# A chain of three layers on one core: when the second feed-forward layer's weights are loaded, joined and stored while the first one runs

## The chip, the cores and the metric

The kernel runs on one core of a Trainium2 chip. The metric is the device time of one execution in microseconds (us). TensorE (PE, with its weight loads as PEld) multiplies matrices, VectorE (DVE), ScalarE (ACT) and GpSimd (POOL) do elementwise work, SyncE (SP) issues nearly all DMAs from one queue, in program order.

## The reference

Three layers follow one another: an attention with positive features, a feed-forward layer with g = h cos h, and a feed-forward layer with g = relu(h)².

```
phi(x)  = concat(exp(p - m), exp(-(p - m)))   with p = x @ w_phi, m = max|p|
attn    = phi(q) (phi(k)^T v) / (phi(q) sum(phi(k)) + 1e-6)     # 4 x 8 heads, 576 tokens of 64
x       = attn as 2304 tokens x 512
h = x @ moe_w_in  (512 -> 2048);  x = (h * cos(h)) @ moe_w_out  (2048 -> 512)
h = x @ moe2_w_in (512 -> 2048);  out = relu(h)**2 @ moe2_w_out (2048 -> 512)
```

All weights of the two feed-forward layers arrive as 64-bit floats, which the chip's engines don't compute with. The kernel reads them as pairs of 32-bit words and makes 32-bit floats of them; those it splits into a high and a low part, and each product is three matmuls (high x high, high x low, low x high).

## The kernel before, in words

**Order of the layers.** Attention fills the first 175 us. The first feed-forward layer follows in five blocks of tokens, of 512, 256, 512, 512 and 512 tokens (blocks 0 to 4). The second feed-forward layer takes the rest; it forms its first product with seven products instead of eight (line 615, its elementwise work from L632 on) and its second one at L670.

**A block of the first layer.** `feed_forward` goes through 16 + 3 steps i. Step i issues G1 of chunk i (12 matmuls, L313 to L315), then elementwise work of chunks i and i-1, then G2 of chunk i-3 (12 matmuls, L385). Elementwise: ScalarE rounds (A1: L327, L328), VectorE reduces the argument (A2: L330, L332), ScalarE takes sine and square (B1: L334, L335), VectorE forms h cos h (B2: L337), ScalarE makes its high part g (B3: L342) and VectorE the low part (B4: L345). `g` has two buffers, freed by G2. At the end of a block `split_x` splits the next block's tokens (L299, L303).

**Conversion of a weight tile** (128 rows x 512 values, 512 KB). A load (L472) brings the words. `w_words` takes the magnitude of one word (ACT, L239, into `mag`, three buffers) and scales the other in place (ACT, L241). `w_join` clamps (DVE, L257), shifts (DVE, L259), adds the two words (POOL, L261) and puts in the sign (DVE, L267). For the first product of the second layer, pairs of tiles are combined to the sums that its seven products want (`combine`, POOL, L511). `spill_split` makes the high part (ACT, L531) and the low part (DVE, L532) in a staging area, and SyncE stores it to DRAM (L533). The second layer reads it back (L493, and `read_out` at L502).

**What sets the order.** Each engine works in program order. `ahead()` lists events for tiles of the second layer, each with a due time `at`: load, words, joins, splits. `converts(j, i)` advances a clock by the matmul time that the step of block j adds (about a microsecond of TensorE per unit; 12 matmuls at 512 columns count 2.72) and, at the end of each step of blocks 1 to 3, issues all events due by then. Twenty tiles are treated so: the 16 of `w_in` and 4 of `w_out`; the other 12 of `w_out` (`late_outs`) are converted during the second layer and stay on chip. Loads alternate between two areas in the upper rows of the buffer `xbuf` (`areas(0)`, `areas(1)`), the staging areas are one slot of the weight pool (`st`) and `areas(2)`, `areas(3)`. Areas 0 and 2, and 1 and 3, lie in the same rows, and a load, a conversion or a split that touches one waits for what still reads or writes the other.

Of the kernel before, what the change touches and what calls it, by code (L numbers as in the profile page):

```python
# [31 lines left out]
AHEAD_TILES = (  # L32
    ("out", 0), ("out", 1), ("in", 0), ("in", 1), ("in", 2), ("in", 3), ("out", 2), *(("in", n) for n in range(4, 8)),
    ("out", 3), *(("in", n) for n in range(8, 16)),
)
AHEAD_FIRST, AHEAD_NEXT, AHEAD_STAGE = (0.0, 11.0, 22.0, 33.0), 9.7, 5.5
# [128 lines left out]
def attention_ffn_kernel(  # L165
# [11 lines left out]
    nc = tc.nc  # L177
# [15 lines left out]
    with tc.manual_schedule():  # L193
# [58 lines left out]
        def w_join(layer, n, step):  # L252
            m = mag_t[layer, n]
            mi = m.bitcast(I32)
            word0, word1 = raw_t[layer, n]
            if step == 0:
                nc.vector.tensor_scalar(out=m, in0=m, scalar1=F64_MIN, scalar2=F64_MAX, op0=ALU.max, op1=ALU.min)  # L257
            elif step == 1:
                nc.vector.tensor_scalar(out=mi, in0=mi, scalar1=3, scalar2=None, op0=ALU.logical_shift_left)  # L259
            elif step == 2:  # L260
                soon(layer, n).tensor_tensor(out=halves(mi), in0=halves(mi), in1=word0, op=ALU.add)  # L261
            else:
                raw_t.pop((layer, n))
# [256 lines left out]
        def spill_split(src, to, at):  # L520
            n = staged[0] % (3 if at >= 47.0 else 1)
# [11 lines left out]
            nc.sync.dma_start(out=to, in_=st[:, :, 0:w])  # L533

        def split_piece(p, i, at):
# [6 lines left out]
            spill_split(src, spilled(p, i), at)  # L542

        def stages(t, at, d, load, split):
            p = t[1] // 2
            yield at - d, lambda: load(t)
            yield at, lambda: [w_words(1, t, i) for i in range(2)]
            yield at + d, lambda: [w_join(1, t, i) for i in range(3)]
            yield at + 2 * d, lambda: w_join(1, t, 3)
            if t[0] == "out":  # L550
                yield at + 3 * d, lambda: split(t, at + 3 * d)
            elif t[1] % 2:
                yield at + 2 * d, lambda: combine(p)
                yield at + 3 * d, lambda: [split_piece(p, i, at + 3 * d) for i in (0, 3)]
                yield at + 4 * d, lambda: [split_piece(p, i, at + 4 * d) for i in (1, 2)]

        def ahead():
            events = []
            for n, t in enumerate(AHEAD_TILES):
                at = AHEAD_FIRST[n] if n < 4 else AHEAD_FIRST[3] + AHEAD_NEXT * (n - 3)  # L560
# [4 lines left out]
                def split(t, at):  # L565
                    spill_split(mag_t.pop((1, t)), out_spill(t[1]), at)

                events += stages(t, at, AHEAD_STAGE, load, split)
            return sorted(events, key=lambda e: e[0])

        def late_outs():
            events = []
            for n in range(4, KFF):
# [4 lines left out]
                def split(t, at):  # L578
                    w_split(1, t, 0)
                    w_split(1, t, 1)  # L580

                events += stages(("out", n), 9 + (n - 4) * 3.0, 2, load, split)
            return sorted(events, key=lambda e: e[0])

# [134 lines left out]
        def second_layer():  # L719
            events = late_outs()  # L720
            for s in range(1, NG * NP + 1):
                for k in range(7):
                    second_step(s, k)
                    while events and events[0][0] < 7 * s + k + 1:
                        events.pop(0)[1]()
# [10 lines left out]
        def behind_last(i):  # L736
# [7 lines left out]
            elif i >= 10 and i % 2 == 0 and i < 18:  # L744
                read_out((i - 10) // 2)
# [386 lines left out]
```

## Time and profile before

| | |
|---|---|
| median of 3 runs | 997.62 us (997.43 to 997.94) |
| profiled execution | 999.31 us, its span 997.5 us |
| TensorE busy | 968.7 us, 97% of the span, 5865 matmuls |
| VectorE, ScalarE, GpSimd busy | 66%, 59%, 17% |
| mean granted clock of TensorE | 0.988 |

TensorE is busy nearly throughout. A busy TensorE at its lower clock does half as much, so its busy share alone doesn't tell what is lost: the profile's slices of the span show 97% busy and a few slices in which busy share or granted clock is 8 tenths, between 270 and 530 us. That is where the first layer's blocks 1 to 3 run with the conversions of the second layer's weights among them. The rows below cover that stretch and what follows it.

### The profile page before, as it was taken

What the parts mean: (1) busy time and instruction counts of PE and PEld (TensorE: products, weight loads), DVE (VectorE), ACT (ScalarE), POOL (GpSimd) and SP (SyncE); (2) the same over time, 40 slices, a digit from 0 to 9 for tenths busy, and PEclk for the clock granted to TensorE, in tenths of its full rate; (3) what the DMA queues carried; (4) which work ended last, traced back from release to release, by engine and by line L of the source; (5) the groups of instructions that cost most, each with busy time, mean ns of one, the idle gap of its engine ahead of it and who ended that gap; (6) DMA issues with size and microseconds to landing.
All of it is one profiled execution on the core that took longest, in us unless ns stands there. A gap on an engine that the chain in (4) does not pass through costs nothing.

```text
span 997.5 us, 15678 instructions
## 1 busy us (share of the span) xinstructions
PE 968.7 (97%) x5865; PEld 831.8 (83%) x5865; DVE 661.7 (66%) x1136; ACT 585.2 (59%) x1145; POOL 171.1 (17%) x146
## 2 busy tenths in 40 slices
PE   8999999999979999899989999999999999999998
PEld 8888888788879788678868888898888888898887
DVE  6787887599846767777676754678774434743444
ACT  4988887699757766776676663455443223432223
POOL 1665863000001223223210000122100000000000
PEclk9999999999989999899989999999999999999999
DMA  7567632322023233354234502765644435453311
GB/s 253 160 203 223 209 106 78 111 105 76 14 72 106 75 139 117 136 168 137 97 141 152 171 1 74 249 205 180 204 147 146 120 118 156 155 166 109 117 53 63
DMA packets 54459, 132.46 MB, mean 133 GB/s; under 512 B 6512, under 2 KB 12272, under 8 KB 54384
## 3 DMA queue, kind: packets, MB, share of 16 engines
q1 hardware_dynamic: 54240, 131.41, 40.8%
q8 instruction: 46, 0.75, 0.3%
q14 instruction: 29, 0.24, 0.1%
q10 hardware_dynamic: 144, 0.07, 0.0%
HBM read 105.09 MB, written 26.29 MB: 132 GB/s over the span
## 4 chain that ended last, share of the span: by engine, by line
PE 45%; DVE 4%; ACT 4%; DMA 2%; issue 1%; POOL 1%; SPq 0%; DVEq 0%; ACTq 0%; POOLq 0%
PE acc L670 19%; PE m L615 17%; PE acc L385 5%; PE h L315 1%; PE h L314 1%; PE h L313 1%; DMA xbuf<-in_dram 1%; DVE tr L330 1%; DMA sp<-xbuf 1%; ACT tr L334 1%; ACT tr L327 1%; ACT tr L328 1%; DVE xr L445 0%; DVE tr L332 0%; DVE xc L452 0%
## 5 line engine op out<-in xcount | busy, mean ns | idle before, releaser
L385 PE MATMUL acc<-g,w 128*128 128x512 f32 (+1 forms) x960 | 221.6, 380 | 18.9 <-ACT g L342 13.6
L670 PE MATMUL acc<-w,g 128*128 128x512 f32 x864 | 226.0, 394 | 0.0
L385 PEld LDWEIGHTS acc<-g,w 128*128 128x128 f32 x960 | 173.1, 195 | 56.5 <-ACT g L342 16.0
L670 PEld LDWEIGHTS acc<-w,g 128*128 128x128 f32 x864 | 159.7, 188 | 23.3
L615 PE MATMUL m<-xc,wc 128*128 128x384 f32 x864 | 174.0, 336 | 2.8 <-DVE t L638 1.7
L615 PEld LDWEIGHTS m<-xc,wc 128*128 128x128 f32 x864 | 154.4, 188 | 16.7 <-DVE t L638 2.6
L313 PE MATMUL h<-xs,w 128*128 128x512 f32 (+1 forms) x320 | 118.8, 371 | 0.0
L314 PE MATMUL h<-xs,w 128*128 128x512 f32 (+1 forms) x320 | 118.4, 370 | 0.0
L315 PE MATMUL h<-xs,w 128*128 128x512 f32 (+1 forms) x320 | 118.3, 370 | 0.0
L597 DVE TENSOR_TENSOR g<-t,g 128x384 fp32r<-128x384 f32 x96 | 53.0, 573 | 71.3 <-ACT g L596 71.2
L337 DVE SCALAR_TENSOR_TENSOR tr<-tr,h 128x512 f32<-128x512 f32 (+1 forms) x80 | 50.5, 632 | 54.7 <-ACT tr L335 54.7
L596 ACT ACTIVATE g<-t 128x384 fp32r<-128x384 f32 x96 | 47.3, 518 | 66.6 <-DVE t L629 66.5
L261 POOL TENSOR_TENSOR mag<-mag,raw 128x512 int32<-128x512 int32 x32 | 42.5, 1327 | 208.6 <-DVE mag L259 182.5
L330 DVE SCALAR_TENSOR_TENSOR tr<-tr,h 128x512 f32<-128x512 f32 (+1 forms) x80 | 50.7, 633 | 38.4 <-ACT tr L328 37.9
L313 PEld LDWEIGHTS h<-xs,w 128*128 128x128 f32 x320 | 61.2, 191 | 10.3 <-issue 0.2
L314 PEld LDWEIGHTS h<-xs,w 128*128 128x128 f32 x320 | 61.1, 191 | 10.1
L315 PEld LDWEIGHTS h<-xs,w 128*128 128x128 f32 x320 | 61.0, 191 | 10.1
L342 ACT ACTIVATE g<-tr 128x512 fp32r<-128x512 f32 (+1 forms) x80 | 46.3, 580 | 32.0 <-DVE tr L332 14.6
L871 PEld LDWEIGHTS kv<-v,e 128*128 128x128 f32 x512 | 60.1, 192 | 3.4 <-ACT e L863 2.0
L871 PE MATMUL kv<-v,e 128*128 128x65 f32 x512 | 62.3, 274 | 0.5 <-ACT e L863 0.3
L261 POOL TENSOR_TENSOR mag<-mag,xbuf 128x512 int32<-128x512 int32 x20 | 28.8, 1440 | 194.9 <-DVE mag L259 118.8
L345 DVE TENSOR_TENSOR g<-tr,g 128x512 fp32r<-128x512 f32 (+1 forms) x80 | 52.7, 659 | 13.2 <-ACT g L342 13.2
(94 smaller groups left out, 1427.1 us busy)
## 6 DMA issues: line engine op xcount, KB each, us to landing
wc<-sp SPq DMA_DIRECT2D x72, 512.0 KB
raw<-in_dram SPq DMA_DIRECT2D x44, 512.0 KB
xbuf<-in_dram SPq DMA_DIRECT2D x20, 512.0 KB
sp<-xbuf SPq DMA_DIRECT2D x17, 512.0 KB
kq<-in_dram SPq DMA_DIRECT2D x16, 384.0 KB
wc<-sp SPq DMA_DIRECT2D x24, 256.0 KB
v<-in_dram SPq DMA_DIRECT2D x16, 330.0 KB
dn<-db SPq DMA_DIRECT2D x32, 144.0 KB
```

The source lines that it names most:

```text
L261: soon(layer, n).tensor_tensor(out=halves(mi), in0=halves(mi), in1=word0, op=ALU.add)
L313: nc.tensor.matmul(out=hps, lhsT=ih[:, kk, :], rhs=xh, start=kk == 0, stop=False)
L314: nc.tensor.matmul(out=hps, lhsT=ih[:, kk, :], rhs=xl, start=False, stop=False)
L315: nc.tensor.matmul(out=hps, lhsT=il[:, kk, :], rhs=xh, start=False, stop=kk == KDM - 1)
L330: nc.vector.scalar_tensor_tensor(out=r, in0=t, scalar=-C1, in1=h_t[c], op0=ALU.mult, op1=ALU.add)
L337: nc.vector.scalar_tensor_tensor(out=t, in0=r, scalar=1.0, in1=h_t.pop(c), op0=ALU.subtract, op1=ALU.mult, reverse0=True)
L345: nc.vector.tensor_tensor(out=g[:, 1], in0=t, in1=f(g[:, 0]), op=ALU.subtract)
L385: nc.tensor.matmul(out=acc[m][:, 0:n], lhsT=l, rhs=r, start=c == 0 and i == 0, stop=c == KFF - 1 and i == 2)
L597: nc.vector.tensor_tensor(out=g[:, 1], in0=t, in1=f(g[:, 0]), op=ALU.subtract)
L615: nc.tensor.matmul(out=m, lhsT=l[:, sl], rhs=r[:, q], start=start and q == 0 and n == 0, stop=q == 1 and n == 2, skip_group_check=True,)
L670: nc.tensor.matmul(out=acc[m], lhsT=g[:, l, sl], rhs=w[:, r], start=p == 0 and f_ == 0 and i == 0, stop=p == NP - 1 and f_ == 1 and i == 2,)
L871: nc.tensor.matmul(out=acc[:, s, h, 0:D + 1], lhsT=e[:, t, s, :], rhs=v_t[u][:, t, h, 0:D + 1], start=t == 0 and h == 0 and s == 0, stop=F ...
```

## The change

Due times of the events change, and with them the program order on all engines but TensorE, whose instructions stay in the same order.

- 18 tiles are converted ahead instead of 20: two of `w_out` and the 16 of `w_in`. The late tiles of `w_out` are 14 instead of 12; they start in step 10 of block 4 instead of in the second layer.
- Words of the first three tiles are due at 12, 23, 34 (before 0, 11, 22), those of each further one 10.0 later (before 9.7). The load is due 10.5 ahead of the words (before 5.5), the joins 7.0 behind them (before 5.5).
- The joins come as one event: clamp, shift, sign, addition (before: clamp, shift, addition, and the sign one stage later).
- Splits come one or two to an event, each store half a stage (3.5) behind its split (before: right behind it).
- The three staging areas rotate from words due at 34 on (before from splits due at 47).

```diff
-AHEAD_TILES = (
-    ("out", 0), ("out", 1), ("in", 0), ("in", 1), ("in", 2), ("in", 3), ("out", 2), *(("in", n) for n in range(4, 8)),
-    ("out", 3), *(("in", n) for n in range(8, 16)),
-)
-AHEAD_FIRST, AHEAD_NEXT, AHEAD_STAGE = (0.0, 11.0, 22.0, 33.0), 9.7, 5.5
+AHEAD_TILES = (("out", 0), ("out", 1), *(("in", n) for n in range(16)))
+AHEAD_FIRST, AHEAD_NEXT, AHEAD_STAGE, AHEAD_LOAD = (12.0, 23.0, 34.0), 10.0, 7.0, 10.5
+LATE_FIRST, LATE_NEXT, LATE_STAGE = 0, 3, 2
...
         def spill_split(src, to, at):
-            n = staged[0] % (3 if at >= 47.0 else 1)
+            n = staged[0] % (3 if at >= 34.0 else 1)
...
-            nc.sync.dma_start(out=to, in_=st[:, :, 0:w])
+            return lambda: nc.sync.dma_start(out=to, in_=st[:, :, 0:w])
...
-        def stages(t, at, d, load, split):
-            p = t[1] // 2
-            yield at - d, lambda: load(t)
+        def stages(t, at, d, lead, load, split):
+            p, sends = t[1] // 2, []
+            yield at - lead, lambda: load(t)
             yield at, lambda: [w_words(1, t, i) for i in range(2)]
-            yield at + d, lambda: [w_join(1, t, i) for i in range(3)]
-            yield at + 2 * d, lambda: w_join(1, t, 3)
+            yield at + d, lambda: [w_join(1, t, i) for i in (0, 1, 3, 2)]
             if t[0] == "out":
-                yield at + 3 * d, lambda: split(t, at + 3 * d)
+                yield at + 2 * d, lambda: sends.append(split(t, at))
+                yield at + 2.5 * d, lambda: sends.pop(0)()
             elif t[1] % 2:
                 yield at + 2 * d, lambda: combine(p)
-                yield at + 3 * d, lambda: [split_piece(p, i, at + 3 * d) for i in (0, 3)]
-                yield at + 4 * d, lambda: [split_piece(p, i, at + 4 * d) for i in (1, 2)]
+                for k, i in ((2.0, 0), (2.0, 3), (3.0, 1), (4.0, 2)):
+                    yield at + k * d, lambda i=i: sends.append(split_piece(p, i, at))
+                    yield at + (k + 0.5) * d, lambda: sends.pop(0)()
...
-            for n in range(4, KFF):
+            for n in range(2, KFF):
...
-                events += stages(("out", n), 9 + (n - 4) * 3.0, 2, load, split)
+                events += stages(("out", n), LATE_FIRST + LATE_NEXT * (n - 2), LATE_STAGE, LATE_STAGE, load, split)
...
-            elif i >= 10 and i % 2 == 0 and i < 18:
-                read_out((i - 10) // 2)
+            elif i in (10, 11):
+                read_out(i - 10)
+            convert_late(i - 12)
```

`convert_late(now)` issues the late events that are due before now + 1; in the second layer it is called at each of the seven parts of a step with 7 s + k. In the changed file the lines up to the conversions stand two or three higher, so L239 is L237 there, L241 is L239, L342 is L339, L472 is L469 and L533 is L530.

**ScalarE at the start of block 1.** Before, the words of the first tile (L239, L241) stand behind A1 (L327, L328) of step 0, in which their load is issued too, ahead of B1 (L334, L335):

```order
L402 ACTIVATE xbuf<-acc_2737 128x512
L327 ACTIVATE tr<-h 128x256
L328 ACTIVATE tr<-tr 128x256
L239 ACTIVATE mag<-xbuf 128x512
L241 ACTIVATE xbuf<-xbuf 128x2x256
L334 ACTIVATE tr<-tr 128x256
L335 ACTIVATE tr<-tr 128x256
L327 ACTIVATE tr<-h 128x256
```

Now, from A1 (L324, L325) of step 5, with B1 (L331, L332) of step 6 behind them:

```order
L324 ACTIVATE tr<-h 128x256
L325 ACTIVATE tr<-tr 128x256
L339 ACTIVATE g<-tr 128x256
L237 ACTIVATE mag<-xbuf 128x512
L239 ACTIVATE xbuf<-xbuf 128x2x256
L331 ACTIVATE tr<-tr 128x256
L332 ACTIVATE tr<-tr 128x256
```

The two instructions on the words moved behind B3 (L339) of step 5; their load, due at 1.5 on the planner's clock, is issued at the end of step 1.

**VectorE, the joins of the first tile.** Before, clamp and shift (L257, L259) stand together and the sign (L267) two steps behind them:

```order
L257 TENSOR_SCALAR mag<-mag 128x512
L259 TENSOR_SCALAR mag<-mag 128x512
L337 SCALAR_TENSOR_TENSOR tr<-tr,h 128x256
L330 SCALAR_TENSOR_TENSOR tr<-tr,h 128x256
L332 SCALAR_TENSOR_TENSOR tr<-tr 128x256
L345 TENSOR_TENSOR g<-tr,g 128x256
L337 SCALAR_TENSOR_TENSOR tr<-tr,h 128x256
L330 SCALAR_TENSOR_TENSOR tr<-tr,h 128x256
L332 SCALAR_TENSOR_TENSOR tr<-tr 128x256
L345 TENSOR_TENSOR g<-tr,g 128x256
L267 SCALAR_TENSOR_TENSOR mag<-xbuf,mag 128x512
```

Now the sign (L264) follows the shift:

```order
L255 TENSOR_SCALAR mag<-mag 128x512
L257 TENSOR_SCALAR mag<-mag 128x512
L264 SCALAR_TENSOR_TENSOR mag<-xbuf,mag 128x512
L334 SCALAR_TENSOR_TENSOR tr<-tr,h 128x256
```

The sign moved ahead of POOL's addition, which follows in the same event.

**SyncE around the end of block 1** (`x_75<-ot` is block 1's result, `sp<-` and `so<-` are stores of split tiles, `xbuf<-in_dram` loads). Before, pairs of loads and groups of stores:

```order
L472 DMA xbuf<-in_dram 128x2x512 x2
L405 DMA x_75<-ot 128x256 x4
L472 DMA xbuf<-in_dram 128x2x512
L533 DMA sp<-xbuf 128x2x512
L533 DMA sp<-st 128x2x256
L533 DMA sp<-xbuf 128x2x512 x2
L472 DMA xbuf<-in_dram 128x2x512 x2
L533 DMA sp<-st 128x1024
L533 DMA sp<-xbuf 128x2x256
L533 DMA sp<-xbuf 128x2x512
```

Now:

```order
L469 DMA xbuf<-in_dram 128x2x512
L402 DMA x_75<-ot 128x256 x4
L469 DMA xbuf<-in_dram 128x2x512
L530 DMA sp<-xbuf 128x2x512
L530 DMA sp<-st 128x2x256
L469 DMA xbuf<-in_dram 128x2x512
L530 DMA sp<-xbuf 128x2x512
L469 DMA xbuf<-in_dram 128x2x512
L530 DMA sp<-xbuf 128x2x512
L530 DMA sp<-st 128x1024
L530 DMA sp<-xbuf 128x2x256
L469 DMA xbuf<-in_dram 128x2x512
```

Loads stand one by one between the stores, and ahead of stores that they followed before.

## Rows read from the trace of the kernel before

**Rows 1.** Waits of TensorE over the whole span: waiter, releaser, us in total, times, longest us.
```profile
PE acc L385 <- ACT g L342: 13.6, 4, 5.5
```

**Rows 2.** Windows along the blocks: length, busy us of each engine (x instructions), granted clock, DMA.
```profile
273.20:300.00 26.80, 20.97 (x151) 20.47 (x150) 12.40 (x30) 15.53 (x40) 1.31 (x1) 0.87 0.23 79
300.00:332.05 32.05, 29.95 (x236) 28.56 (x235) 22.53 (x51) 22.53 (x57) 3.93 (x3) 1.00 0.25 83
332.05:400.00 67.95, 67.90 (x301) 55.89 (x300) 48.11 (x81) 48.69 (x88) 18.20 (x18) 1.00 0.38 126
400.00:430.53 30.53, 24.84 (x88) 18.64 (x87) 22.11 (x36) 19.49 (x35) 6.62 (x7) 0.83 0.44 152
430.53:495.00 64.47, 64.44 (x284) 53.05 (x283) 47.00 (x75) 45.29 (x80) 17.29 (x18) 1.00 0.39 131
495.00:526.50 31.50, 26.66 (x103) 20.76 (x102) 22.52 (x36) 21.41 (x38) 6.47 (x7) 0.89 0.32 117
526.50:605.40 78.90, 78.90 (x350) 65.33 (x349) 51.85 (x74) 51.18 (x84) 0.00 (x0) 1.00 0.34 101
605.40:700.00 94.60, 93.50 (x466) 83.81 (x465) 63.22 (x112) 44.03 (x87) 13.56 (x10) 1.00 0.59 187
```

**Rows 3.** Timeline in block 4: start, duration, engine, line, operation, tiles, count [idle before <-releaser].
```profile
586.34 2.88 PE L385 MATMUL acc<-g,w 128*128 128x512 f32 x12
...
591.78 2.88 PE L385 MATMUL acc<-g,w 128*128 128x512 f32 x12
```

**Rows 4.** Timeline near the end of block 1, width 256.
```profile
313.28 0.42 DVE L332 SCALAR_TENSOR_TENSOR tr<-tr 128x256 f32<-128x256 f32 x1
...
313.69 1.60 PE L385 MATMUL acc<-g,w 128*128 128x256 f32 x12
...
315.57 1.32 POOL L261 TENSOR_TENSOR mag<-mag,xbuf 128x512 int32<-128x512 int32 x1 [10.63 <-DVE mag L259]
...
316.13 1.04 DVE L332 SCALAR_TENSOR_TENSOR tr<-tr 128x256 f32<-128x256 f32 x1
...
316.57 1.60 PE L385 MATMUL acc<-g,w 128*128 128x256 f32 x12
...
319.27 0.66 ACT L239 ACTIVATE mag<-xbuf 128x512 f32<-128x512 f32 x1 [2.99 <-DMA xbuf<-in_dram]
```

**Rows 5.** Timeline at the start of block 1.
```profile
277.46 1.80 SPq L472 DMA_DIRECT2D xbuf<-in_dram  x2
...
281.55 0.66 ACT L239 ACTIVATE mag<-xbuf 128x512 f32<-128x512 f32 x1 [5.88 <-DMA xbuf<-in_dram]
...
284.58 0.58 PE L385 MATMUL acc<-g,w 128*128 128x256 f32 x1 [5.46 <-ACT g L342]
...
285.52 2.72 PE L385 MATMUL acc<-g,w 128*128 128x256 f32 x11 [0.36 <-DVE g L345]
```

**Rows 6.** Timeline in the last third of block 2.
```profile
410.19 0.67 ACT L239 ACTIVATE mag<-xbuf 128x512 f32<-128x512 f32 x1 [3.89 <-DMA xbuf<-in_dram]
...
414.30 0.79 PE L385 MATMUL acc<-g,w 128*128 128x512 f32 x1 [2.84 <-ACT g L342]
```

**Rows 7.** Waits of ScalarE from 275 to 535, same columns as Rows 1.
```profile
ACT mag L239 <- DMA xbuf<-in_dram: 21.9, 8, 5.9
ACT tr L334 <- DVE tr L332: 17.0, 21, 1.5
ACT xbuf L531 <- POOL mag L261: 16.6, 5, 3.6
ACT g L342 <- DVE tr L337: 10.7, 13, 2.2
...
ACT xbuf L241 <- DMA sp<-xbuf: 3.6, 3, 2.9
```

**Rows 8.** Lines by form from 275 to 535: xcount | busy us, mean ns | idle before.
```profile
L261 POOL TENSOR_TENSOR mag<-mag,xbuf 128x512 int32<-128x512 int32 x20 | 28.8, 1440 | 194.9 <-DVE mag L259 118.8 <-ACT tr L327 69.7 <-ACT tr L334 6.3
...
L267 DVE SCALAR_TENSOR_TENSOR mag<-xbuf,mag 128x512 int32<-128x512 int32 x20 | 13.7, 683 | 0.0
```

More of the change, by code (lines that the diff above doesn't have):

```diff
@@ L262, in w_join @@
             else:
-                raw_t.pop((layer, n))
                 if layer == 0:
@@ L541, in split_piece @@
                 src = wc["f"][:, 2 * i - 2:2 * i]
-            spill_split(src, spilled(p, i), at)
-        def stages(t, at, d, load, split):
-            p = t[1] // 2
-            yield at - d, lambda: load(t)
+            return spill_split(src, spilled(p, i), at)
+        def stages(t, at, d, lead, load, split):
+            p, sends = t[1] // 2, []
+            yield at - lead, lambda: load(t)
             yield at, lambda: [w_words(1, t, i) for i in range(2)]
-            yield at + d, lambda: [w_join(1, t, i) for i in range(3)]
-            yield at + 2 * d, lambda: w_join(1, t, 3)
+            yield at + d, lambda: [w_join(1, t, i) for i in (0, 1, 3, 2)]
             if t[0] == "out":
-                yield at + 3 * d, lambda: split(t, at + 3 * d)
+                yield at + 2 * d, lambda: sends.append(split(t, at))
+                yield at + 2.5 * d, lambda: sends.pop(0)()
             elif t[1] % 2:
                 yield at + 2 * d, lambda: combine(p)
-                yield at + 3 * d, lambda: [split_piece(p, i, at + 3 * d) for i in (0, 3)]
-                yield at + 4 * d, lambda: [split_piece(p, i, at + 4 * d) for i in (1, 2)]
+                for k, i in ((2.0, 0), (2.0, 3), (3.0, 1), (4.0, 2)):
+                    yield at + k * d, lambda i=i: sends.append(split_piece(p, i, at))
+                    yield at + (k + 0.5) * d, lambda: sends.pop(0)()
         def ahead():
-            events = []
+            events, last = [], len(AHEAD_FIRST) - 1
             for n, t in enumerate(AHEAD_TILES):
-                at = AHEAD_FIRST[n] if n < 4 else AHEAD_FIRST[3] + AHEAD_NEXT * (n - 3)
+                at = AHEAD_FIRST[min(n, last)] + AHEAD_NEXT * max(n - last, 0)
                 def load(t, n=n):
@@ L565, in split @@
                 def split(t, at):
-                    spill_split(mag_t.pop((1, t)), out_spill(t[1]), at)
-                events += stages(t, at, AHEAD_STAGE, load, split)
+                    return spill_split(mag_t.pop((1, t)), out_spill(t[1]), at)
+                events += stages(t, at, AHEAD_STAGE, AHEAD_LOAD, load, split)
             return sorted(events, key=lambda e: e[0])
@@ L580, in split, with convert_late @@
                     w_split(1, t, 1)
-                events += stages(("out", n), 9 + (n - 4) * 3.0, 2, load, split)
+                    return lambda: None
+                events += stages(("out", n), LATE_FIRST + LATE_NEXT * (n - 2), LATE_STAGE, LATE_STAGE, load, split)
             return sorted(events, key=lambda e: e[0])
+        late_events = late_outs()
+        def convert_late(now):
+            while late_events and late_events[0][0] < now + 1:
+                late_events.pop(0)[1]()
         def quarter(s, name):
@@ L723, in second_layer @@
                     second_step(s, k)
-                    while events and events[0][0] < 7 * s + k + 1:
-                        events.pop(0)[1]()
+                    convert_late(7 * s + k)
         def share(j, i):
```

1 line of the change is left out of this document (removed).

## The prediction

> **What bounds the kernel now.** I read four views in this order. First the waits of TensorE [rows 1]: of its waits, 13.6 us are for the high part of g (ScalarE's L342) in only 4 stalls, the longest 5.5, at L385, which is the first layer's second product. Then the table of windows [rows 2], laid along the blocks. Block 1 runs from 273.20 to 332.05, block 2 to 430.53, block 3 to 526.50, block 4 to 605.40. The reader is to see that the stretches from 332.05 to 400 and from 430.53 to 495 are full (TensorE busy 67.90 of 67.95 and 64.44 of 64.47, granted clock 1.00), that block 4, in which nothing of the second layer's weights is converted, is full too (78.90 of 78.90), and that the loss stands in three stretches: 273.20 to 300 (clock 0.87), 400 to 430.53 (0.83), 495 to 526.50 (0.89).
>
> How much is lost there follows from the full rate. In block 4 a step comes every 591.78 − 586.34 = 5.44 us [rows 3], at width 256 every 316.57 − 313.69 = 2.88 us [rows 4]; a step is 24 matmuls (12 of each product), so one takes 0.227 and 0.120 us. A block has 16 steps: ideal 46.08 us for block 1, 87.04 us for blocks 2 and 3. Against their windows 58.85, 98.48 and 95.97 that is a loss of 12.8 + 11.4 + 8.9 = 33.1 us. By stretch, with the counts in [rows 2]: 26.80 − 151 × 0.120 = 8.7; 32.05 − 236 × 0.120 = 3.7; 30.53 − 88 × 0.227 = 10.6; 31.50 − 103 × 0.227 = 8.2 (matmuls that straddle a border count twice, hence the smaller sum of 31.2). These four waits explain 13.6 of it; most of the rest is TensorE at the lower of its two levels (1.2 instead of 2.4 GHz) after each stall: in [rows 5] eleven matmuls take 2.72 us where [rows 4] shows twelve in 1.60.
>
> Then the timeline, for why ScalarE is late. In [rows 5] SyncE issues two loads at 277.46, ScalarE's L239 needs the first at once and has waited 5.88 us for it at 281.55; L334, L335 and L342 of the block's first step stand behind it in ScalarE's order, and TensorE starts L385 5.46 us late. In [rows 6] L239 waits 3.89 us at 410.19, and L385 2.84 us at 414.30. Last the waits of ScalarE over the stretch [rows 7]: 21.9 us in 8 waits for loads, 16.6 us in 5 for POOL's addition, 3.6 us for stores that still read the staging area; beside them 17.0 and 10.7 us for VectorE, which are the loop's own latency.
>
> A budget says why the sum spills. ScalarE is busy 38.1 + 68.2 + 66.7 = 173.0 us in the three blocks [rows 2], whose ideal time is 220.2: 47.2 us are free. Its waits listed are 69.8 us. What exceeds the room, 22.6 us, has to come out as a stall.
>
> **The change part by part.** Durations are from the profiled execution, which took 999.31 us (span 997.5 and 1.8 around it); the median of the three runs is 997.62, 1.7 lower. I sum against the first and shift the result by 1.7.
>
> *First words later, load lead 10.5 instead of 5.5.* Only 18 tiles instead of 20 are converted in blocks 1 to 3, and the first words move from step 0 of block 1 to step 5, while the load is issued at the end of step 1. The landing of 277.46 to 281.55 = 4.1 us [rows 5] then lies beside four steps, one of them with only the first product: 1.44 + 3 × 2.88 = 10.1 us. The first stall goes: −8.7 (ends: 0 if something else holds L239 as long; −8.7). What is late next there is nothing but the loop. For the other loads the same lead covers the longest wait, 5.9 us [rows 7], on top of the old lead: 5.0 units of the planner's clock more (a unit is about a microsecond of TensorE). The loads of 410.19 (3.89) and of block 1's end (2.99 at 319.27, [rows 4]) are then there in time: 21.9 us of ScalarE's waits fall to about 0 (ends 0 and 21.9). A load is issued in SyncE's order only when the addition on the tile two before has freed its area; behind it in SyncE's queue stand the stores, so a load that waits holds them back.
>
> *Sign ahead of the addition.* Work is unchanged: clamp and shift as before, 0.683 us sign and 1.44 addition [rows 8]. The addition starts 0.68 later in its step, but it is now the last thing, with two half-stages until the split where before only the sign's step lay between. Where split and addition still fall into one step (four places by the order of the instructions: three in block 2, one at block 3's end) ScalarE waits as before, up to 3.6 us [rows 7]: 4 × 3.6 = 14.4 in place of 16.6 (ends: 4 × 4.3 = 17.2 with the sign's 0.68 added; 0).
>
> *Stores half a stage later, three staging areas earlier.* A store no longer waits at SyncE's head for VectorE, and loads pass it. Reuse of an area waits for a landing; I book 5 places at 0.4 = 2 us in place of 3.6 (ends: 0, and 5 × 2.9 = 14.5, the longest of [rows 7] each time).
>
> By the budget ScalarE's waits become 27.7 (loop) + 0 + 14.4 + 2 = 44.1 of 47.2 us free: it fits, with 3 us to spare. As the lag is local and block 2 holds three of the four places, I leave 2.0 of the 33.1 us standing (0.5 at the end of blocks 1 and 2 each, 1 at the start of block 3).
>
> One thing speaks against it. VectorE's L332 at width 256 takes 0.42 us at 313.28 and 1.04 at 316.13, beside POOL's addition from 315.57 to 316.89 [rows 4]: 0.62 us dearer. The Trainium skill ("SBUF — State Buffer", section "Who interferes with whom") states that a VectorE instruction with two SBUF inputs and a GpSimd instruction that reads SBUF exclude one another for the whole instruction; the trace agrees in kind. By that rule each of 18 additions could hold VectorE for its whole 1.44 us, an estimate of 26 us from this case's duration, 15 more than by the row; 12 of them over the room, and in proportion to 33.1 us for 22.6 a loss of 17.6: 985. By the row alone it is 18 × 0.62 = 11 us, and as 20 additions cost it before, it is inside the loop's 27.7: I take it as unchanged, and it is a reason for rival A.
>
> *Two more tiles among the late ones, starting in block 4.* One tile costs ScalarE three instructions and VectorE four; taken at L239's 0.66 [rows 5] and L267's 0.68 each, with POOL's 1.44, its chain is 2.0 + 2.7 + 1.4 = 6.1 us (an estimate). In block 4 ScalarE is idle 78.90 − 51.18 = 27.7 us, VectorE 27.0, POOL all of it; behind it, to 700, ScalarE is idle 50.6 us and TensorE loses 1.1 [rows 2]. Bounds −1.1 (that loss goes) and 2 × 6.1 = +12.2 (both chains wholly on the path); I take +0.5, near the low end, because idle time covers it. Two stores and two read-backs less: 0, they were not waited for.
>
> Sum: −33.1 + 2.0 + 0.5 = −30.6; 999.31 − 30.6 = 968.7, as a median 967.0 us.
>
> **The rivals.**
> (A) One or two stalls remain: ScalarE's lag at the three additions in one step of block 2 adds to the interference above, and L385 waits there. One stall with its stretch at the lower level cost 8.2 us (495 to 526.50): 967.0 + 8.2 = 975; with two, 983. For it: only 3 us of room. Against it: block 2 ran 68 us with the same additions without a loss.
> (B) The lead brings nothing in blocks 2 and 3, since the loads are still held at SyncE behind work that is late: then only block 1's 8.7 + 3.7 go: 985.2. For it: a load waits for the addition two tiles back, which now is due only 20 − 7 − 10.5 = 2.5 units ahead of it (before 2 × 9.7 − 5.5 − 5.5 = 8.4), half a step. Against it: what counts is the distance to the words, which is 10.5 units, or two steps of 5.44 us, against a landing of 4.1.
> (C) Slower. Each load now stands ahead of stores in SyncE's one queue and waits there for POOL; stores and then staging areas and loads are late by turns, so that each of the 18 loads makes ScalarE wait. With a wait of t each, its waits are 27.7 + 14.4 + 18t; they equal the old 69.8 at t = 1.5 us, from which it decides. At the mean of the waits seen, 21.9/8 = 2.7, they are 90.7, an excess of 43.5 against 22.6; in proportion the loss is 33.1 × 43.5/22.6 = 63.7, or 997.6 + 30.6 = 1028. Against it: 10.5 − 4.1 = 6.4 us of slack that a late addition would have to eat up first, 18 times.
> (D) The edit does nothing in sum: stalls move to other steps with the same total, 997.6.
>
> **How the numbers follow.** Forecast 0.62, A 0.22, B 0.08, D 0.04, C 0.04. The range goes from 963.5 (all 33.1 us and the 1.1 behind block 4 gone: 963.4) to 983 (A with two stalls); B, C and D, 16 in 100, lie outside. No change means within 0.2%, 2 us, about what a measurement of this kernel can tell: only D. Slower is C. All else is faster: 0.92.
>
> **What would show it.** Right: no wait of some microseconds at L239 after block 1 begins; the window of block 1 near 46.6, of block 2 near 87.5, of block 3 near 88, granted clock 1.00 in all; TensorE's waits at L385 for g under 2 us in sum; block 4 and the second layer as long as before. The sign's step is wrong if ScalarE's waits for POOL at the hi copies (L531) grow over 17 us; the stores' step if waits for stores at the word conversions grow over 3.6. A block 2 above 94 us would be A, loads still awaited for some 20 us in sum B, over 27 us C; block 4 longer than 80 us would refute the term of the late tiles.

## The result, and the profile after

The changed kernel takes 973.87 us (972.08 to 974.5, 4 runs) against 997.78 us in the runs beside it (997.43 to 997.99, 4 runs): a ratio of 0.9758, 95% interval 0.9741 to 0.9775, or 23.9 us less. The forecast was 967.0 us, range 963.5 to 983. The direction and most of the gain are as forecast; 7 us that should have gone are still there, and, as the experiments show, part of the reasons given were wrong, so that the near hit is in part luck.

The windows along the blocks of the profiled execution after (block starts from the first matmul of each; columns as in [rows 2]; the last two windows are block 4 and the stretch behind it):

```profile
273.04:322.56 49.52, 47.39 (x386) 46.38 (x384) 34.35 (x79) 36.81 (x94) 3.91 (x3) 1.00 0.25 87
322.56:412.86 90.30, 88.29 (x387) 71.83 (x385) 67.31 (x111) 66.59 (x119) 24.40 (x24) 1.00 0.40 128
412.86:501.58 88.72, 87.65 (x386) 71.99 (x384) 69.00 (x111) 65.92 (x116) 24.11 (x23) 1.00 0.38 132
501.58:580.48 78.90, 78.90 (x350) 65.33 (x349) 52.62 (x76) 52.16 (x86) 1.31 (x1) 1.00 0.36 114
580.48:675.00 94.52, 93.42 (x464) 83.32 (x463) 68.51 (x121) 48.26 (x94) 16.41 (x12) 1.00 0.59 187
```

Block 1 went from 58.85 to 49.52 us, block 2 from 98.48 to 90.30, block 3 from 95.97 to 88.72 [rows 2]: 9.3 + 8.2 + 7.2 = 24.8 us, which is the whole difference of the spans (997.5 and 972.7). From block 4's start to the end it takes 471.1 us as against 471.0, with two tiles more to convert. The granted clock is 1.00 in every block: no wait that is left is followed by a stretch at the lower level. Over the full rate (46.08, 87.04, 87.04) are left 3.4 + 3.3 + 1.7 = 8.4 us; the forecast had left 2.0.

TensorE's waits for g over the whole span (columns as in [rows 1]): first, from before, the row for the low part, which [rows 1] doesn't have, then both rows after, where L339 is the former L342 and L342 the former L345:

```profile
PE acc L385 <- DVE g L345: 5.0, 10, 1.0
```

```profile
PE acc L382 <- DVE g L342: 4.5, 8, 1.0
...
PE acc L382 <- ACT g L339: 0.8, 1, 0.8
```

The 13.6 us for the high part of g [rows 1] are 0.8; what is left are eight waits of at most 1.0 us for VectorE's low part, of which there were ten before. ScalarE's waits from 275 to 510 show what it was late for:

```profile
ACT xbuf L528 <- POOL mag L259: 15.5, 4, 4.6
ACT tr L331 <- DVE tr L329: 14.9, 19, 1.5
ACT g L339 <- DVE tr L334: 10.4, 12, 1.4
...
ACT xbuf L239 <- DVE xbuf L529: 2.5, 1, 2.5
...
ACT xbuf L239 <- DMA sp<-xbuf: 1.0, 2, 0.5
```

The row for loads, 21.9 us in [rows 7], is gone. The high copy (L528) still waits four times for POOL's addition, 15.5 us in place of 16.6: twice in block 2 (ending at 347.96 and 360.01) and twice in block 3 (416.28 and 481.75).

### The profile page after: what moved, and what is told of

The parts are those of the page before. It is cut to its first block, busy times and chain, and to the rows that moved or that the text cites. A ratio compares the mean times of both kernels' runs of the same rounds, so it can differ in the third digit from the quotient of the medians.

```text
span 972.7 us, 15694 instructions
## 1 busy us (share of the span) xinstructions
PE 956.6 (98%) x5865; PEld 823.6 (85%) x5865; DVE 664.9 (68%) x1136; ACT 584.9 (60%) x1145; POOL 172.4 (18%) x146
## 4 chain that ended last, share of the span: by engine, by line
PE 72%; DVE 13%; ACT 8%; issue 3%; DMA 2%; POOL 0%; SPq 0%; DVEq 0%; ACTq 0%; POOLq 0%
PE acc L675 19%; PE m L620 17%; PE acc L382 12%; PE kv L875 4%; PE h L310 4%; PE h L312 4%; PE h L311 4%; PE nm L921 2%; PE pj L841 2%; DVE tr L329 2%; ACT tr L325 2%; ACT tr L324 2%; PE nm L929 1%; DVE tr L327 1%; PE tp L898 1%
## 5 line engine op out<-in xcount | busy, mean ns | idle before, releaser
L382 PE MATMUL acc<-g,w 128*128 128x512 f32 (+1 forms) x960 | 211.7, 370 | 5.4 <-DVE g L342 4.5
L382 PEld LDWEIGHTS acc<-g,w 128*128 128x128 f32 x960 | 167.9, 188 | 39.0 <-DVE g L342 7.3
L259 POOL TENSOR_TENSOR mag<-mag,raw 128x512 int32<-128x512 int32 x34 | 45.4, 1335 | 205.9 <-DVE mag L264 134.2
L327 DVE SCALAR_TENSOR_TENSOR tr<-tr,h 128x512 f32<-128x512 f32 (+1 forms) x80 | 50.6, 633 | 36.7 <-ACT tr L325 36.3
L334 DVE SCALAR_TENSOR_TENSOR tr<-tr,h 128x512 f32<-128x512 f32 (+1 forms) x80 | 50.5, 631 | 31.6 <-ACT tr L332 31.6
L312 PEld LDWEIGHTS h<-xs,w 128*128 128x128 f32 x320 | 60.4, 189 | 10.1
L310 PEld LDWEIGHTS h<-xs,w 128*128 128x128 f32 x320 | 60.4, 189 | 10.0 <-issue 0.2
L311 PEld LDWEIGHTS h<-xs,w 128*128 128x128 f32 x320 | 60.3, 189 | 10.0
L339 ACT ACTIVATE g<-tr 128x512 fp32r<-128x512 f32 (+1 forms) x80 | 46.3, 580 | 35.7 <-DVE tr L329 14.6
L342 DVE TENSOR_TENSOR g<-tr,g 128x512 fp32r<-128x512 f32 (+1 forms) x80 | 53.3, 667 | 13.7 <-ACT g L339 13.7
L856 DVE TENSOR_REDUCE m<-pj 128x4 f32<-128x512 f32 (+1 forms) x80 | 49.9, 623 | 16.5 <-PE pj L841 9.2
```

What stands on the lines that cost most here:

```text
L310: nc.tensor.matmul(out=hps, lhsT=ih[:, kk, :], rhs=xh, start=kk == 0, stop=False)
L311: nc.tensor.matmul(out=hps, lhsT=ih[:, kk, :], rhs=xl, start=False, stop=False)
L312: nc.tensor.matmul(out=hps, lhsT=il[:, kk, :], rhs=xh, start=False, stop=kk == KDM - 1)
L327: nc.vector.scalar_tensor_tensor(out=r, in0=t, scalar=-C1, in1=h_t[c], op0=ALU.mult, op1=ALU.add)
L334: nc.vector.scalar_tensor_tensor(out=t, in0=r, scalar=1.0, in1=h_t.pop(c), op0=ALU.subtract, op1=ALU.mult, reverse0=True)
L342: nc.vector.tensor_tensor(out=g[:, 1], in0=t, in1=f(g[:, 0]), op=ALU.subtract)
```

## The experiments

Each kernel was timed in three rounds beside the kernel before (996 to 1000 us in all of them). The lengths of the blocks come from the starts of their first matmuls; "behind" is the span from block 4's start to the end. Lengths are those of one profiled execution, which in c12 took 989.8 us and in u3 976.8, others within 0.9 us of the time shown or, for before, 1.5. Block 1 starts between 272.05 and 273.21 us in all of them, with no edit ahead of it; lengths of blocks tell more than differences of 1 us in the whole.

| kernel | time, us | ratio (95% interval) | block 1 | block 2 | block 3 | behind |
|---|---|---|---|---|---|---|
| before | 997.8 | 1 | 58.9 | 98.5 | 96.0 | 471.0 |
| changed | 973.9 | 0.976 (0.974, 0.978) | 49.5 | 90.3 | 88.7 | 471.1 |
| e1, before with lead 10.5 | 1012.2 | 1.015 (1.013, 1.017) | 57.5 | 105.9 | 103.5 | 471.0 |
| u1, changed, lead 5.5 | 974.0 | 0.977 (0.976, 0.979) | 49.5 | 90.3 | 88.6 | 470.9 |
| u2, changed, sign a stage later | 985.9 | 0.989 (0.987, 0.990) | 51.8 | 97.8 | 90.5 | 471.8 |
| u3, changed, stores at once | 978.0 | 0.981 (0.979, 0.983) | 49.5 | 93.3 | 89.0 | 470.9 |
| u4, changed, first words at 0 | 980.0 | 0.982 (0.981, 0.984) | 55.1 | 90.3 | 88.7 | 471.0 |
| c13, u1 and u3 together | 988.2 | 0.990 (0.989, 0.992) | 49.6 | 102.9 | 90.7 | 471.6 |
| c12, lead 5.5, sign a stage later | 986.5 | 0.989 (0.988, 0.991) | 51.4 | 101.5 | 90.7 | 471.7 |
| c4, lead 5.5, sign half a stage later | 978.5 | 0.981 (0.980, 0.982) | 47.5 | 92.8 | 88.1 | 476.2 |
| o1, changed, addition then sign | 994.0 | 0.996 (0.994, 0.997) | 54.0 | 100.0 | 91.0 | 475.8 |
| i1, changed, splits first | 969.6 | 0.971 (0.970, 0.973) | 49.5 | 87.3 | 87.0 | 471.2 |
| i2, i1 and joins apart | 966.3 | 0.968 (0.967, 0.970) | 47.7 | 87.2 | 87.0 | 470.9 |
| i3, i1 and one tile more late | 974.7 | 0.976 (0.974, 0.978) | 48.5 | 88.6 | 91.7 | 471.5 |

**e1: the lead alone.**

```diff
-            yield at - d, lambda: load(t)
+            yield at - (10.5 if d > 2 else d), lambda: load(t)
```

> The kernel before with one edit: the load due 10.5 ahead of the words instead of 5.5. Theory (the loads were ScalarE's main avoidable wait, 21.9 us in 8 waits): the waits for loads fall from 21.9 to under 7 us (only the first tile's, whose words stay in step 0 of block 1, remains at some 5.9), the stalls of 400 to 430 and 495 to 526 go for the most part, and the time falls by 12 to 20 us, to 978 to 986 us. Rival (loads are held in SyncE's queue behind stores and additions, so that an earlier place alone brings little): waits for loads stay above 15 us and the time stays above 992 us.

Measured: 1012.2 us, 15 us slower than the runs beside it (997.1). Both theories fell. ScalarE's waits for loads did shrink, to one of 5.3 us; but a load now comes 10.5 units ahead of its words, that is 8.9 units (19.4 − 10.5) behind the words of the tile two before, whose sign is taken 11 behind them. The load overwrites the words that this sign reads, and VectorE, in order, waits at the sign until it has landed (in this kernel and in u2 signs are therefore taken from words of another tile; only the times are read). VectorE's waits from 275 to 560, then ScalarE's from 275 to 540:

```profile
DVE mag L267 <- DMA xbuf<-in_dram: 37.6, 14, 5.3
```

```profile
ACT mag L239 <- DMA xbuf<-in_dram: 5.3, 1, 5.3
```

So the longer lead can't be had with the sign two stages behind the words: in the changed order all joins must be done 20 − 10.5 = 9.5 units behind the words, and at 7.0 they are. What counts here is the sign's due time, not whether it stands ahead of the addition (o1 below has the lead with the sign behind the addition at 7.0).

**u1, u3, c13: lead and late stores, each and both undone.**

```diff
-AHEAD_FIRST, AHEAD_NEXT, AHEAD_STAGE, AHEAD_LOAD = (12.0, 23.0, 34.0), 10.0, 7.0, 10.5
+AHEAD_FIRST, AHEAD_NEXT, AHEAD_STAGE, AHEAD_LOAD = (12.0, 23.0, 34.0), 10.0, 7.0, 5.5
```

> The changed kernel with the load lead set back to 5.5. Theory: waits for loads return on most tiles with 1 to 4 us each, and 8 us or more of the 24 us gained are lost: 982 us or longer. Rival (the gain came from the first words' later place, the sign and the stores): the time stays within 2 us of 974.

```diff
-                yield at + 2.5 * d, lambda: sends.pop(0)()
+                yield at + 2 * d, lambda: sends.pop(0)()
...
-                    yield at + (k + 0.5) * d, lambda: sends.pop(0)()
+                    yield at + k * d, lambda: sends.pop(0)()
```

> The changed kernel with each store issued right behind its split again. Theory (stores waiting at the head of SyncE's queue delay loads by some us, and the longer lead has slack for that): within 2 us of 974. Rival (the later stores are what lets the loads through): waits for loads of 5 us or more in sum return, and the time is 978 us or longer.

> The changed kernel with the lead set back to 5.5 and each store right behind its split. Setting back the lead alone cost nothing, the stores alone 4 us. Theory now (the two stand in for one another: a load gets past SyncE's queue either because it is issued early or because no store that waits for VectorE stands ahead of it): waits for loads come back with 8 us or more in sum and the time is 984 us or longer. Rival (neither matters beyond the stores' 4 us): 978 within 1.5 us.

Measured: the lead undone 974.0 (rival right), the stores undone 978.0, both undone 988.2: 0.1, 4.1 and 14.3 us above the changed kernel (u1 and the changed kernel agree within what such runs can tell, and in every block). The two stand in for one another, as the theory for c13 had it: with the stores at once the lead is worth 10.2 us (c13 to u3), with the later stores nothing. For u3 the time is the rival's, but its reason is not: ScalarE waits for no load there. ScalarE's waits for loads, first in u1, then in c13 (from 275 to 510 and to 520):

```profile
ACT mag L237 <- DMA xbuf<-in_dram: 3.4, 2, 2.3
```

```profile
ACT mag L237 <- DMA xbuf<-in_dram: 21.3, 8, 4.0
```

21.3 us in 8 waits are close to what [rows 7] shows for the kernel before (21.9 in 8, the first tile's 5.9 among them, which c13 doesn't have). The timeline of c13 in block 2 shows how they come about (columns as in [rows 3]):

```profile
401.67 8.83 SPq L530 DMA_DIRECT2D sp<-xbuf  x2
...
409.42 0.69 DVE L529 TENSOR_TENSOR xbuf<-mag,xbuf 128x512 fp32r<-128x512 f32 x1
...
410.02 0.42 DVE L529 TENSOR_TENSOR st<-mag,st 128x256 fp32r<-128x256 f32 x1
...
410.59 0.42 SPq L530 DMA_DIRECT2D sp<-st  x1
411.14 0.81 SPq L469 DMA_DIRECT2D xbuf<-in_dram  x1
415.90 0.67 ACT L237 ACTIVATE mag<-xbuf 128x512 f32<-128x512 f32 x1 [4.00 <-DMA xbuf<-in_dram]
...
419.79 4.86 PE L382 MATMUL acc<-g,w 128*128 128x512 f32 x12 [3.01 <-ACT g L339]
```

SyncE's queue stands at stores that wait for VectorE's low copies (L529); the load behind them is issued at 411.14 and its words are wanted at once. Twelve matmuls behind it take 4.86 us instead of 2.88: the lower clock again (granted clock 0.50 from 420.0 to 423.4). With the stores half a stage later, loads that fall due in between are issued ahead of a store whose low copy isn't done; with the longer lead, the load stands ahead of those stores anyway. Either cures it. In u3 what is left is a store itself, whose landing the word scaling awaits (ScalarE, 275 to 515; 1.0 in the changed kernel):

```profile
ACT xbuf L239 <- DMA sp<-xbuf: 6.3, 3, 5.3
```

**u2, c12, c4, o1: the sign's place.**

```diff
-            yield at + d, lambda: [w_join(1, t, i) for i in (0, 1, 3, 2)]
+            yield at + d, lambda: [w_join(1, t, i) for i in (0, 1, 2)]
+            yield at + 2 * d, lambda: w_join(1, t, 3)
```

> The changed kernel with the sign put back behind the addition, one stage (7.0) later, ahead of combination and split. Theory (the order of sign and addition hardly matters; the joins of 1.5 us in one piece on VectorE cost about what the earlier readiness brings): within 2 us of 974. Rival (having the sign done early is what frees areas and shortens the split's wait): 978 us or longer; second rival (the three VectorE instructions in one piece, which delay the next step's h cos h, are what is left of the loss at the ends of blocks 1 and 2): 972 us or shorter.

> The changed kernel with the lead set back to 5.5 and the sign behind the addition by a stage of 7.0; with that lead the next load of an area again follows the sign that reads it, so that the sign waits for no load. Theory (the sign's place has no worth of its own; it only makes the longer lead possible): within 2 us of 974. Rival (it is what takes VectorE's work out of the split's step): 980 us or longer.

c4 has `(1.5 if d > 2 else 1) * d` in place of `2 * d`:

> The changed kernel with the lead set back to 5.5 and the sign behind the addition again, but only half a stage (3.5) behind it, so that it falls into a step before the split. A full stage behind, it cost 12.7 us, with 16.4 us of waits of the high copy for VectorE's sign. Theory now (what the sign's place is worth is that the split finds the tile finished; the order of sign and addition is worth nothing): those waits fall under 2 us and the time is 973 to 977 us. Rival (the order itself matters, since a load waits for the last reader of its area and that is now the sign on the busier VectorE, or since sign and addition collide): 980 us or longer.

o1 turns two numbers:

```diff
-            yield at + d, lambda: [w_join(1, t, i) for i in (0, 1, 3, 2)]
+            yield at + d, lambda: [w_join(1, t, i) for i in (0, 1, 2, 3)]
```

> The changed kernel with nothing but the order of the last two joins turned: clamp, shift, addition, sign, still in one event at 7.0, with the lead of 10.5. Theory (where the addition is not followed by a step's pause, VectorE stops at the sign until POOL has added, about 1.3 us for each of 18 tiles, and h cos h of the next step stands behind it): waits of VectorE for POOL at the sign of 15 us or more in sum, and the time rises by 4 to 12 us, to 978 to 986 us. Rival (VectorE has room for it in nearly every step): within 2 us of 974.

Measured: u2 985.9 and c12 986.5, so that both theories, that this place of the sign costs nothing, fell. In u2 the load comes ahead of the sign again, as in e1, but that is the smaller part: VectorE waits 9.6 us for loads at the sign, while the sign falls into the split's step and the high copy waits 21.8 us for it (u2, 275 to 520, VectorE's row, then ScalarE's):

```profile
DVE mag L264 <- DMA xbuf<-in_dram: 9.6, 7, 3.1
```

```profile
ACT xbuf L528 <- DVE mag L264: 17.7, 8, 3.8
...
ACT st L528 <- DVE mag L264: 4.1, 2, 2.6
```

In c12 no load comes ahead of the sign, the wait of the high copy stays, and so does the time (ScalarE, 275 to 520):

```profile
ACT xbuf L528 <- DVE mag L264: 13.2, 8, 2.2
...
ACT st L528 <- DVE mag L264: 3.2, 2, 1.6
```

Half a stage behind (c4), the time is 978.5, between theory and rival. Blocks 1 to 3 take 228.4 us together against 228.5 in the changed kernel, though 6.4 us of that wait remain: block 1, where only two joins now stand in one piece, is 2.0 us shorter, block 2 2.5 longer. Its 4.6 us more stand behind block 3 (476.2 against 471.1), where I had put the late tiles' sign directly behind the addition. So within the blocks the place half a stage behind is as good in sum. Directly behind the addition is the dear one: o1 loses 20.2 us of the 23.9. VectorE's waits there from 275 to 535, and one of them in the timeline:

```profile
DVE mag L264 <- POOL mag L259: 27.2, 18, 1.6
```

```profile
352.46 1.30 POOL L259 TENSOR_TENSOR mag<-mag,xbuf 128x512 int32<-128x512 int32 x1 [7.51 <-DVE mag L257]
353.80 0.69 DVE L264 SCALAR_TENSOR_TENSOR mag<-xbuf,mag 128x512 int32<-128x512 int32 x1 [1.41 <-POOL mag L259]
354.52 0.63 ACT L528 ACTIVATE xbuf<-xbuf 128x512 fp32r<-128x512 f32 x1 [2.74 <-DVE mag L264]
```

VectorE stops at each of the 18 signs for 1.5 us (27.2/18), with the next step's h cos h behind it; ScalarE waits 28.9 us for that (10.4 in the changed kernel). The theory was right, its price (4 to 12 us) too low: 16.5 us in the blocks, 4.7 behind them.

**u4: first words at 0.**

```diff
-AHEAD_FIRST, AHEAD_NEXT, AHEAD_STAGE, AHEAD_LOAD = (12.0, 23.0, 34.0), 10.0, 7.0, 10.5
+AHEAD_FIRST, AHEAD_NEXT, AHEAD_STAGE, AHEAD_LOAD = (0.0, 23.0, 34.0), 10.0, 7.0, 10.5
```

> The changed kernel with only the first tile's words (and, 10.5 ahead, its load) set back from 12 to 0. Theory (the first stall of block 1 is the price of words that stand in the same step as their load): the wait of some 5.9 us at the word conversion in step 0 and a stall of some 5 us at the second product return, and the time rises by 8.7 us to about 982.5. Rival (ScalarE has room there now, as the load is alone in SyncE's queue): under 977.

Measured: 980.0, block 1 longer by 5.6 us, and the stall is back in the timeline as in [rows 5], with the windows of block 1 below:

```profile
276.05 1.80 SPq L469 DMA_DIRECT2D xbuf<-in_dram  x2
280.15 0.66 ACT L237 ACTIVATE mag<-xbuf 128x512 f32<-128x512 f32 x1 [5.36 <-DMA xbuf<-in_dram]
283.18 0.58 PE L382 MATMUL acc<-g,w 128*128 128x256 f32 x1 [4.94 <-ACT g L339]
```

```profile
272.33:300.00 27.67, 22.37 (x172) 21.87 (x171) 14.42 (x34) 15.93 (x41) 1.31 (x1) 0.88 0.25 87
300.00:327.42 27.42, 26.17 (x216) 25.77 (x215) 19.93 (x46) 21.23 (x53) 2.60 (x2) 1.00 0.24 70
```

The mechanism is shown; its worth is 5.6 to 6.1 us, not 8.7. What moved out of the way are the words, not the load: SyncE, before, holds the first loads until block 0's result, stored from the same buffer, has landed (its own waits, 270 to 300), and the first load goes out at 277.46 before and at 277.33 in the changed kernel.

```profile
SPq L472 <- DMA x<-xbuf: 3.4, 2, 2.9
```

**i1, i2, i3: what is left.** i1 issues the splits that are due in a step ahead of everything else due in it:

```diff
-                while ahead_events and ahead_events[0][0] < clock[0]:
-                    ahead_events.pop(0)[1]()
+                due = [e for e in ahead_events if e[0] < clock[0]]
+                del ahead_events[:len(due)]
+                for e in sorted(due, key=lambda e: len(e) == 2):
+                    e[1]()
```

(the events of splits carry a third entry, so that they sort first).

> The changed kernel with the splits that fall due in a step issued ahead of everything else due in that step, so that no high copy stands behind an addition of the same step. Theory (ScalarE's 15.5 us in 4 waits at the high copy for POOL are most of what is left of the loss in blocks 2 and 3, 3.3 and 1.7 us over the full rate): these waits fall under 4 us and the time falls by 2 to 4 us, to 970 to 972. Rival (these waits lie in room that ScalarE has, the rest comes from VectorE's late low part of g at the ends of blocks 1 and 2): the waits go and the time stays within 1 us of 974.

Measured: 969.6 us. The high copy's waits for POOL are gone from ScalarE's list, block 2 takes 87.3 and block 3 87.0 us, the full rate (columns as in [rows 2]):

```profile
322.52:409.81 87.29, 87.29 (x386) 72.02 (x385) 70.51 (x111) 68.17 (x121) 26.05 (x24) 1.00 0.41 132
409.81:496.85 87.04, 87.04 (x385) 72.10 (x384) 70.48 (x111) 65.47 (x115) 23.80 (x23) 1.00 0.39 134
```

So having the splits behind the additions, with those four waits, cost 4.7 us of the 5.0 left in these blocks.

i2 puts clamp and shift into an event of their own:

```diff
-            yield at + d, lambda: [w_join(1, t, i) for i in (0, 1, 3, 2)]
+            yield at + 0.6 * d, lambda: [w_join(1, t, i) for i in (0, 1)]
+            yield at + d, lambda: [w_join(1, t, i) for i in (3, 2)]
```

> The kernel with the splits first in a step, and clamp and shift due 2.8 ahead of sign and addition, in a step of their own. The splits first gave 969.6 us; 3.4 us over the full rate are left, nearly all at the end of block 1, where 1.5 us of VectorE's joins stand in one piece ahead of h cos h. Theory (the piece is what is late there): 968 to 969 us. Rival (ScalarE's words and high copies in steps of 2.88 us have used up the room by then, whoever comes last): within 0.5 us of 969.6, or longer.

Measured: 966.3 us (965.7 to 966.6), the fastest of all, 31.6 us below its runs of the kernel before and 1.7 below the theory's range; block 1 fell from 49.5 to 47.7. That is 1.9 of the 3.3 us against i1; 0.9 of the rest stand ahead of block 1, where nothing was edited. What it removes is seen in the changed kernel at the end of block 1:

```profile
317.77 0.42 DVE L255 TENSOR_SCALAR mag<-mag 128x512 f32<-128x512 f32 x1
...
318.23 0.43 DVE L257 TENSOR_SCALAR mag<-mag 128x512 int32<-128x512 int32 x1
318.69 0.69 DVE L264 SCALAR_TENSOR_TENSOR mag<-xbuf,mag 128x512 int32<-128x512 int32 x1
319.30 0.41 DVE L334 SCALAR_TENSOR_TENSOR tr<-tr,h 128x256 f32<-128x256 f32 x1
...
319.80 0.42 ACT L339 ACTIVATE g<-tr 128x256 fp32r<-128x256 f32 x1 [1.38 <-DVE tr L334]
...
320.27 0.39 PE L382 MATMUL acc<-g,w 128*128 128x256 f32 x1 [0.79 <-ACT g L339]
321.14 1.58 PE L382 MATMUL acc<-g,w 128*128 128x256 f32 x11 [0.48 <-DVE g L342]
```

Three joins, 1.5 us in one piece, stand ahead of h cos h (L334) in a step of 2.88 us; ScalarE waits 1.38 and TensorE 0.79 + 0.48 us. The blocks of i2, columns as in [rows 2]:

```profile
272.08:319.73 47.65, 46.97 (x386) 46.30 (x384) 33.08 (x79) 36.86 (x94) 3.94 (x3) 1.00 0.26 90
319.73:406.89 87.16, 87.16 (x387) 72.02 (x385) 69.00 (x111) 68.11 (x121) 24.76 (x24) 1.00 0.42 133
406.89:493.93 87.04, 87.04 (x386) 72.10 (x384) 69.41 (x111) 65.33 (x115) 23.45 (x23) 1.00 0.39 134
```

i3 is i1 with the second tile of `w_out` moved to the late ones (its read-back in block 4 goes too):

```diff
-AHEAD_TILES = (("out", 0), ("out", 1), *(("in", n) for n in range(16)))
-AHEAD_FIRST, AHEAD_NEXT, AHEAD_STAGE, AHEAD_LOAD = (12.0, 23.0, 34.0), 10.0, 7.0, 10.5
+AHEAD_TILES = (("out", 0), *(("in", n) for n in range(16)))
+AHEAD_FIRST, AHEAD_NEXT, AHEAD_STAGE, AHEAD_LOAD = (12.0, 34.0), 10.0, 7.0, 10.5
...
-            for n in range(2, KFF):
+            for n in range(1, KFF):
```

> The kernel with the splits first in a step and the second tile of w_out moved to the late ones (15 instead of 14, its conversion begins in block 4), so that block 1 converts one tile fewer. Theory (the last 3.4 us are too much conversion work for the steps of 2.88 us of block 1, and block 4 has room for one tile more): the waits at the end of block 1 go, block 4 stays as long as it is, 966 to 967.5 us. Rival (block 4 or the first steps of the second layer have no room left for a third tile): block 4 longer by 1 us or more and the time above 969 us.

Measured: 974.7 us. Against i1, block 1 got only some 1 us shorter, and the stretch behind block 3 0.3 longer, so the rival's reason is wrong as well; block 2 takes 88.6 in place of 87.3, and most of the loss stands in block 3 (91.7 in place of 87.0), early in it:

```profile
418.75 0.67 ACT L239 ACTIVATE xbuf<-xbuf 128x512 int32<-128x512 uint32 x1 [2.85 <-DMA x<-xbuf]
...
422.32 0.50 PE L382 MATMUL acc<-g,w 128*128 128x512 f32 x1 [1.40 <-ACT g L339]
423.85 4.39 PE L382 MATMUL acc<-g,w 128*128 128x512 f32 x11 [1.03 <-DVE g L342]
```

ScalarE's scaling of words waits 2.85 us there for a store of block 2's result, which leaves from the same buffer (0.43 at that place in i1), and the eleven matmuls run at a granted clock of 0.62 (423.85 to 428.40). With one tile less every later tile of `w_in` takes the other load area and falls into other steps; which of the two brought the wait about was not tried.

**What no run undoes.** Two tiles fewer in blocks 1 to 3, the spacing of 10.0, the stage of 7.0 and the earlier use of three staging areas were not undone by themselves. Lead and stores together are worth 14.3 us and the first words 6.1; as far as they add, these are 20.4 of the 23.9 us, and what the other parts gave is open.

## Why the prediction was right or wrong, point by point

- *Where the loss stood, and that conversions made it*: right. The three blocks gave back 24.8 us, nothing else changed by more than 0.2, and i2 shows that nearly all of the 33.1 us can be had.
- *First words later, −8.7*: the mechanism was right, the size wrong: 6 us (u4). With the first stall (u4) block 1 takes 55.1 us, 9.0 over the full rate, without it 3.4. Up to 300 us u4 loses 27.67 − 172 × 0.120 = 7.0 us where I had 8.7, and behind it 27.42 − 216 × 0.120 = 1.5 us: the stall itself was smaller with the rest of the change in place, and block 1's end loses less behind a stall, so the two losses, which I had counted as independent, aren't.
- *The lead takes 21.9 us of waits away*: the waits went, but not through the lead, which is worth nothing that can be told from noise in the changed kernel (u1, 0.1 us). My reason against rival B, that the distance from load to words is what counts, failed: what counts is whether stores that wait for VectorE stand ahead of the load in SyncE's queue. The edit that I booked at a saving of 1.6 us of waits, the later stores, cures it as well as the lead; without both, 14.3 us return (c13). That the largest term came true in spite of its wrong reason is luck: another edit in the same change did its work. Rival B's 8.4 units before were wrong too. They were counted from the addition, but the last reader of the words was then the sign, due 11 behind them: 19.4 − 5.5 − 11 = 2.9 units, against 2.5 now.
- *Sign ahead of the addition, "work is unchanged"*: I weighed 0.68 us of delay. Against an addition directly in front of it the order is worth 20 us (o1). A sign that is done by 9.5 units behind the words is the condition for the lead (e1). Half a stage behind the addition and with the shorter lead, the sign is as good in the blocks in sum (c4); in the split's step, a whole stage behind, it costs 12 us (c12).
- *Four high copies in the addition's step, 4 × 3.6 = 14.4*: measured 15.5 in four waits, so the term was right in sum; the places were two in block 2 and two in block 3, not three and one. The whole budget came out: loop 14.9 + 10.4, additions 15.5, areas 2.5 + 1.0, together 44.3 us where I had 44.1. The step that failed is the one behind it: "it fits, with 3 us to spare". A budget over three blocks can't say that: each of these waits (up to 4.6 us) falls on one step of 5.44 us, and there they cost 4.7 us (i1). By place I had allowed 1.5 us for blocks 2 and 3.
- *Stores and areas, 2 us of waits*: 1.0 for stores, and 2.5 in one wait for VectorE's low copy, which I had not put. Without the later stores it is 6.3 and the time 4.1 us more (u3), so the term was small only with them.
- *Block 1's end, 0.5 us*: block 1 is 3.4 over the full rate. The load's wait at 319.27 [rows 4] went, but three joins in one event took its place; I had not put them as a term. Taking them apart gave 1.9 us in block 1 (i2), and c4, which takes one of them out of the piece, 2.0. With i1 and i2 together 1.7 of the 8.4 us are left.
- *The interference of VectorE and POOL*: still there. L329 (the former L332) of width 256 takes 1.13 us in the changed kernel beside an addition, 0.43 without:

```profile
307.94 1.31 POOL L259 TENSOR_TENSOR mag<-mag,xbuf 128x512 int32<-128x512 int32 x1 [7.47 <-DVE mag L264]
307.95 0.42 DVE L327 SCALAR_TENSOR_TENSOR tr<-tr,h 128x256 f32<-128x256 f32 x1
...
308.40 1.13 DVE L329 SCALAR_TENSOR_TENSOR tr<-tr 128x256 f32<-128x256 f32 x1
...
311.65 0.43 DVE L329 SCALAR_TENSOR_TENSOR tr<-tr 128x256 f32<-128x256 f32 x1
```

  It ends 0.28 us behind the addition (309.53 against 309.25), just as in [rows 4] (317.17 against 316.89). So VectorE is held until the addition ends, as the prediction's rule has it, but what that costs is only what remains of the addition when VectorE's instruction comes; the 26 us took the whole of it each time. That it would stay inside the loop's waits held: these are 14.9 and 10.4 us, 17.0 and 10.7 before [rows 7], and i2 reaches the full rate in blocks 2 and 3 in spite of it.
- *Late tiles, +0.5*: 0.1 or less (471.0 us from block 4's start before, 471.1 after). The idle time covers them as long as VectorE doesn't stop at a sign (o1 and c4: 4.7 and 5.1 us).
- *Rivals*: by the time alone A with one stall (975) is nearer to the 973.9 than the forecast (967.0), and ScalarE's lag at the additions, which it names, is what i1 removes. Its mark, block 2 above 94 us, was not reached, nor its full stall with the lower clock; what is left are nine short waits. B, C and D didn't happen as kernels, but B's mechanism (loads behind late stores) is real and is what c13 shows.
- *The marks*: block 1 was to be near 46.6, 2 near 87.5, 3 near 88; they are 49.5, 90.3 and 88.7. The clock (1.00), the loads and TensorE's waits for the high part (0.8, under 2) came as said.

## What to carry to other kernels

In a queue that issues in order, look at what stands ahead of a late transfer and what that waits for, before you lengthen its lead; later stores may do the same. Ahead of a longer lead, find the last reader of the buffer that it fills: its place decides whether the lead is a gain (10.2 us, c13 to u3) or a loss (15 us, e1). And a budget of idle time over a long stretch is only an upper bound: which instructions share a step, and in what order each engine finds them, decided 6.6 of the 8.4 us that the change left (i1, i2).

## What was not expected of the hardware

In these runs the lower clock came with the few long waits, and the many short ones hardly changed. Before, TensorE's waits for g were 18.6 us in fourteen: four for the high part, 13.6 us, the longest 5.5, and ten for the low part, 5.0 us, none above 1.0. The granted clock was 0.83 to 0.89 in the three stretches in which the loss stood [rows 1, 2], and the loss 33.1 us. After, they are nine, 5.3 us in sum, none above 1.0, with a loss of 8.4 us at a granted clock of 1.00.

A VectorE instruction whose two inputs both lie in SBUF, the engines' on-chip memory (L329, the former L332), and that comes during one of POOL's additions ends a fixed time after it, 0.28 us at width 256 in both rows shown, so that an early one is held longer than a late one. L327, one of whose inputs is TensorE's result h, took 0.42 us beside the same addition at 307.95.
